# Six small GpSimd loads into a tile without readers, in an attention and GEGLU decode kernel

## The chip, the cores and the metric

The kernel runs on one core of a Trainium2 chip. The metric is device time in microseconds (us). The median of three runs of the kernel before is 188.51 us (188.46 to 188.59). The profile shows one separate execution of the same kernel.

The engines are PE (TensorE, the matrix engine), DVE (VectorE), ACT (ScalarE), POOL (GpSimd) and SP (SyncE). In the profile PEld is PE's weight load, and SPq, POOLq and so on are an engine's sequencer, which waits and issues DMAs. Data moves between the off-chip memory and the on-chip memory (128 partitions) through 16 DMA engines.

## The reference

One decode step of a transformer block for two sequences: a modulation computed from a condition `c`, attention of one query over the last 1024 cached positions with 32 heads of 192, and a gated feed-forward part. Weights, inputs and caches are bf16.

```python
mod = (silu(c) @ w_mod).reshape(2, 6, 1, 640)       # sa, ca, ga, sb, cb, gb
h = layernorm(x) * (1 + ca) + sa
q = (h @ wq).reshape(2, 1, 32, 192).transpose(0, 2, 1, 3)
k, v = k_cache[:, :, -1024:], v_cache[:, :, -1024:]  # each [2, 32, 1024, 192]
p = softmax(einsum('bhqd,bhkd->bhqk', q, k) * 192 ** -0.5)
x = x + ga * (einsum('bhqk,bhkd->bhqd', p, v) reshaped @ wo)
h = layernorm(x) * (1 + cb) + sb
x = x + gb * ((gelu(h @ w_gate) * (h @ w_up)) @ w_down)
```

## The kernel before, in words

The program writes one list of operations for each engine, in the order in which they are declared; a small scheduler (`_Sched`) adds the waits. `S.op` declares a computing operation and `S.dma` a load or a store. Each takes the keys that it reads and writes, and further dependencies in `deps`; from these, `emit` puts semaphore waits (line 93) in front of an instruction. A DMA adds 16 in all to its semaphore when it has landed. All DMAs are declared for SP, and the DMA call itself is the helper `k_dma`, so that all of them carry line 261.

The work goes through these stages:

- The modulation matrix `w_mod` (4800 KB on the page), the small inputs `c` and `x` (eight rows of 320 bytes each, into the tiles `cc` and `xc`), and `wq` in two pieces are loaded. POOL clears some tiles and builds an identity matrix (lines 270 to 281), and after that has no work. The query is computed and broadcast into the tile `qbc`.
- K and V stream through a ring of five slots. A load fills a slot with one tile: 128 partitions of 64 rows of 192, 24,576 bytes in a partition. There are four tiles of K and four of V for each sequence, in the order K of sequence 0; then V of sequence 0 and K of sequence 1 by turns; then V of sequence 1. `declare_ring` declares a load as soon as the slot's previous tile has its last reader, and that reader is what SP waits for.
- A step `(b, t, hf)` handles half a tile of K: DVE multiplies it in place by the query (`d_mul`, line 456), PE sums groups of products with the identity matrix (`p_reduce`, line 467), and DVE adds up the rest (`d_rows`, line 476). PE also runs `filler` products (line 445) whose results nobody reads. After sequence 0's K come its softmax (lines 482 to 499), masks (`d_mask`, line 504) and products with V (`p_pv`, line 516), the latter two in between the steps of sequence 1.
- Then the output projection (`wo`, four loads into the place of `wq`), the second normalisation and the feed-forward part. `w_gate`, `w_up` (two loads) and `w_down` (three loads) go into ring slots, behind the last readers of those.
- The result is stored, and SP's tail waits for the store.

The loop around the change declares the steps; `keep[("red", b, t)]` is the latest `p_reduce` of a tile. The tile `cc` is read once, by the SiLU on ACT (line 351, at 14.5 us in the profile).

Of the kernel before, what the change touches and what calls it, by code (L numbers as in the profile page):

```python
# [103 lines left out]
def bass_adaLN_cond__sliding_block_cached__geglu_ffn__decode_kernel(  # L104
# [15 lines left out]
    P = 128  # L120
# [11 lines left out]
    DN = D // NJ  # L132
# [39 lines left out]
    with es:  # L172
        S = _Sched(nc, es)
# [35 lines left out]
        cc = sb("cc", [P, DN], BF16)  # L209
# [36 lines left out]
        def bank(k):  # L246
            return ("bank", k)
# [8 lines left out]
        sem_wd = [S.sem("d_wd%d" % i) for i in range(len(WD_SPLIT))]  # L256
        sem_ring = [S.sem("d_ring%d" % i) for i in range(NS)]
        sem_out = S.sem("d_out")

        def k_dma(dst, src):  # L260
            return lambda e: e.dma_start(dst, src)  # L261
# [45 lines left out]
        def half_key(slot, hf):  # L307
            return ("ring", slot, hf)
# [4 lines left out]
        keep = {}  # L313
# [16 lines left out]
        def slot_of(*it):  # L330
            return place[it] % NS

        def declare_ring(*consumed, upto=len(items)):
            ring_state["done"].update(place[it] for it in consumed)
            while ring_state["next"] < upto and (ring_state["next"] < NS or (ring_state["next"] - NS) in ring_state["done"]):
                n = ring_state["next"]
                kind, b, t = items[n]
                slot = n % NS
                cache = A_v_cache if kind == "v" else A_k_cache
                S.dma("sp", k_dma(ring[:, slot, :, :].rearrange("p j d -> p (j d)"),  # L340
                                  cache[b, :, K0:Sk, :].rearrange("h (q r) d -> h q r d", q=QP)[:, :, J * t:J * (t + 1), :].rearrange("h q r d -> h q (r d)")),
                      sem_ring[slot], writes=ring_keys(slot), name="ld_%s%d_%d" % (kind, b, t))
                ring_state["next"] += 1
# [107 lines left out]
        def filler(n=1):  # L451
            warm(n * ND, BK_W)

        def d_mul(b, t, hf):
            ks = slot_of("k", b, t)
            S.op("dve", lambda e: e.tensor_tensor(out=ring[:, ks, hf * JH:(hf + 1) * JH, :], in0=ring[:, ks, hf * JH:(hf + 1) * JH, :],  # L456
                                                  in1=qbc[:, b, :].unsqueeze(1).broadcast_to([P, JH, Dh]), op=ALU.mult),
                 reads=["qbc"], writes=[half_key(ks, hf)], name="mul%d_%d_%d" % (b, t, hf))

        def p_reduce(b, t, hf):  # L460
            ks = slot_of("k", b, t)

            def f(e):
                last = None
                o_ap = ps[:, hf, 0:JH * GC].rearrange("p (j c) -> p j c", j=JH)
                for ci in range(NCH):
                    last = e.matmul(o_ap, lhsT=ident_b[:, :], rhs=ring[:, ks, hf * JH:(hf + 1) * JH, ci * GC:(ci + 1) * GC],  # L467
                                    start=(ci == 0), stop=(ci == NCH - 1))
                return last
            keep[("red", b, t)] = S.op("pe", f, reads=[half_key(ks, hf), "ident_b"], writes=[bank(hf)], name="red%d_%d_%d" % (b, t, hf))  # L470
            if hf == 1:
                declare_ring(("k", b, t))

        def d_rows(b, t, hf):
            a = J * t + JH * hf
            S.op("dve", lambda e: e.tensor_reduce(out=S_sb[:, a:a + JH], in_=ps[:, hf, 0:JH * GC].rearrange("p (j c) -> p j c", j=JH),  # L476
                                                  axis=AX.X, op=ALU.add),
                 reads=[bank(hf)], writes=[("S", t, hf)], name="rows%d_%d_%d" % (b, t, hf))
# [24 lines left out]
        def d_mask(b, t):  # L503
            S.op("dve", lambda e: e.tensor_tensor(out=Em[:, t % 2, :, :], in0=E_sb[:, J * t:J * (t + 1)].unsqueeze(2).broadcast_to([P, J, H]),  # L504
                                                  in1=M32b[:, :].unsqueeze(1).broadcast_to([P, J, H]), op=ALU.mult),
                 reads=["E", "M32b"], writes=[("Em", t % 2)], name="mask%d_%d" % (b, t))

        def p_pv(b, t):
            vs = slot_of("v", b, t)
            n = J // 2  # L510

            def f(e):
                last = None
                for jp in range(n):
                    r = 2 * SQ * (jp % 2)
                    last = e.matmul(ps[r:r + 2 * H, BK_O, 0:ON],  # L516
                                    lhsT=Em[:, t % 2, 2 * jp:2 * jp + 2, :].rearrange("p j c -> p (j c)"),
                                    rhs=ring[:, vs, 2 * jp:2 * jp + 2, :],
                                    start=(t == 0 and jp < 2), stop=(t == NTL - 1 and jp >= n - 2), tile_position=(0, r), skip_group_check=True)
                return last  # L520
            keep["pv"] = S.op("pe", f, reads=[("Em", t % 2)] + ring_keys(vs), writes=[bank(BK_O)], name="PV%d_%d" % (b, t))
            declare_ring(("v", b, t))
# [22 lines left out]
            S.op("pe", f, reads=["SEL"] + [("On", b, g) for g in range(NJ)], writes=[bank(BK_H + c) for c in range(NQC)], name="sel%d" % b)  # L545

        steps = [(b, t, hf) for b in range(2) for t in range(NTL) for hf in range(2)]
        for n, (b, t, hf) in enumerate(steps):
            if b == 1 and hf == 0:
                if t == 0:  # L550
                    d_rows(*steps[n - 1])
                    softmax(0)
                d_mask(0, t)
            d_mul(b, t, hf)
            if b == 1 and hf == 0:
                p_pv(0, t)
            filler()
            p_reduce(b, t, hf)
            if n > 0 and not (b == 1 and t == 0 and hf == 0):
                d_rows(*steps[n - 1])  # L560
        normalize(0)
# [24 lines left out]
        for i, (ta, tb) in enumerate(wo_of):  # L586
# [5 lines left out]
              writes=["wg"], deps=r3_dead, name="ld_wg")  # L592
# [72 lines left out]
        with nc.Block() as block:  # L665
            def sp_tail(e):
                e.wait_ge(sem_out, 16)

            @block.sync
            def _(e):  # L670
                S.emit("sp", e, tail=sp_tail)

            @block.gpsimd
            def _(e):
                S.emit("pool", e)

            @block.scalar
            def _(e):
                S.emit("act", e)

            @block.vector
            def _(e):
                S.emit("dve", e)

            @block.tensor
            def _(e):
                S.emit("pe", e)
# [28 lines left out]
```

## Time and profile before

| | |
|---|---|
| median of 3 runs | 188.51 us (188.46 to 188.59) |
| profiled execution, its own time | 188.72 us |
| its span, first to last instruction | 187.0 us |
| instructions in the span | 2330 |
| mean granted clock of PE | 0.896 |
| busy: PE, DVE, ACT, POOL | 126.3, 107.0, 13.9, 4.9 us |
| read from off-chip memory | 76.88 MB, 411 GB/s over the span |
| DMA packets | 4221, of which 500 under 512 bytes |

The profile's page divides the span into 40 equal slices (4.7 us each) and gives the busy share of each engine in tenths, and of the 16 DMA engines together. Its table of queues gives packets, megabytes, and the packets' time as a share of 16 engines' span. The chain of work that ended last is followed back from the last instruction to whatever released each piece. The windows give busy time in chosen stretches, and the timeline single instructions: start in us, length in us, engine, line, operation, output and inputs. Besides these views the trace records every DMA packet (queue, start, length, bytes) and every update of a semaphore by a DMA, so that one load's landing can be seen as up to 16 moments, one for each DMA engine that took part.

### The profile page before, as it was taken

What the parts mean: (1) busy time and instruction counts of PE and PEld (TensorE: products, weight loads), DVE (VectorE), ACT (ScalarE), POOL (GpSimd) and SP (SyncE); (2) the same over time, 40 slices, a digit from 0 to 9 for tenths busy, and PEclk for the clock granted to TensorE, in tenths of its full rate; (3) what the DMA queues carried; (4) which work ended last, traced back from release to release, by engine and by line L of the source; (5) the groups of instructions that cost most, each with busy time, mean ns of one, the idle gap of its engine ahead of it and who ended that gap; (6) DMA issues with size and microseconds to landing.
All of it is one profiled execution on the core that took longest, in us unless ns stands there. A gap on an engine that the chain in (4) does not pass through costs nothing.

```text
span 187.0 us, 2330 instructions
## 1 busy us (share of the span) xinstructions
PE 126.3 (68%) x1039; PEld 62.6 (34%) x1039; DVE 107.0 (57%) x114; ACT 13.9 (7%) x24; POOL 4.9 (3%) x12
## 2 busy tenths in 40 slices
PE   0004542564999899449999829929719999688663
PEld 0001221251443343125454414503315555455321
DVE  6802500029799997399699198296564540744331
ACT  2003300031000000100000000000010001400400
POOL 8100000000000000000000000000000000000000
PEclk9999999558799999957999988975975999999998
DMA  7999899999999999999999999999999999999980
GB/s 263 394 474 426 386 450 424 415 442 457 426 431 417 424 421 426 436 452 431 431 419 421 431 426 421 452 435 431 421 421 431 426 435 429 416 402 437 410 360 27
DMA packets 4221, 77.02 MB, mean 412 GB/s; under 512 B 500, under 2 KB 500, under 8 KB 1140
## 3 DMA queue, kind: packets, MB, share of 16 engines
q1 hardware_dynamic: 4212, 76.88, 96.6%
q8 instruction: 8, 0.13, 0.3%
q14 instruction: 1, 0.01, 0.0%
HBM read 76.88 MB, written 0.00 MB: 411 GB/s over the span
## 4 chain that ended last, share of the span: by engine, by line
DMA 47%; PE 27%; DVE 21%; SPq 2%; issue 1%; ACT 1%; POOL 0%; POOLq 0%; DVEq 0%
DMA ring<-in_A_k_cache_dram 34%; DVE ring L456 14%; DMA ring<-in_B_w_down_dram 13%; PE ps L516 11%; PE ps L467 11%; PE ps L445 3%; DVE Sg L476 3%; DVE Em L504 2%; SPq L261 2%; ACT E_sb L495 1%; DVE M L482 0%; PE ps L497 0%; PE ps L491 0%; DVE gm L486 0%; PE ps L484 0%
## 5 line engine op out<-in xcount | busy, mean ns | idle before, releaser
L456 DVE TENSOR_TENSOR ring<-ring,qbc 128x6144 bf16<-128x6144 bf16 x16 | 53.5, 3351 | 11.6 <-DMA ring<-in_A_k_cache_dram 11.6
L467 PE MATMUL ps<-ring,ident_b 128*128 128x512 bf16 x192 | 49.9, 416 | 12.5 <-DVE ring L456 12.5
L467 PEld LDWEIGHTS ps<-ring,ident_b 128*128 128x128 bf16 x192 | 19.3, 105 | 40.0 <-DVE ring L456 16.3
L516 PE MATMUL ps<-ring,Em 128*64 128x384 bf16 x256 | 26.7, 371 | 4.9 <-DVE Em L504 4.9
L445 PE MATMUL ps<-qbc,ident_b 128*128 128x384 bf16 x145 | 28.8, 331 | 0.7 <-ACT qbc L423 0.7
L504 DVE TENSOR_TENSOR Em<-E_sb,M32b 128x2048 bf16<-128x2048 bf16 x8 | 18.2, 2282 | 4.7 <-PE ps L516 4.7
L516 PEld LDWEIGHTS ps<-ring,Em 128*64 128x64 bf16 x256 | 15.6, 125 | 15.4 <-DVE Em L504 6.4
L445 PEld LDWEIGHTS ps<-qbc,ident_b 128*128 128x128 bf16 x145 | 13.2, 100 | 13.6 <-issue 5.0
L476 DVE TENSOR_REDUCE Sg<-ps 128x32 f32<-128x512 f32 x16 | 11.0, 686 | 9.0 <-PE ps L467 9.0
L392 PE MATMUL ps<-ring,scT 128*32 128x480 bf16 x40 | 4.4, 601 | 15.3 <-DVE scT L349 15.3
L415 PE MATMUL ps<-r,hT 128*32 128x384 bf16 x80 | 6.2, 488 | 9.1 <-DMA r<-in_A_wq_dram 9.1
L425 DVE CAST ring<-ps 128x384 bf16<-128x384 f32 x4 | 2.0, 552 | 15.3 <-PE ps L415 14.4
L415 PEld LDWEIGHTS ps<-r,hT 128*32 128x32 bf16 x80 | 2.9, 135 | 12.5 <-issue 5.8
L530 ACT ACTIVATE On<-ps,rden 32x192 bf16<-32x192 f32 x4 | 1.6, 411 | 73.1 <-PE ps L516 62.3
L392 PEld LDWEIGHTS ps<-ring,scT 128*32 128x32 bf16 x40 | 1.2, 132 | 16.7 <-DVE scT L349 15.3
L611 PE MATMUL ps<-r,ring 128*32 128x160 bf16 x192 | 4.1, 233 | 2.8 <-DVE ring L580 1.1
L534 DVE TENSOR_SCALAR On<-ps,rden 32x192 bf16<-32x192 f32 x4 | 1.7, 417 | 7.4 <-ACT On L530 7.4
L611 PEld LDWEIGHTS ps<-r,ring 128*32 128x32 bf16 x192 | 3.4, 97 | 3.9 <-issue 2.7
L580 DVE STREAM_TRANSPOSE ring<-ring 128x512 bf16<-128x512 bf16 x3 | 4.1, 1424 | 0.1
L495 ACT ACTIVATE E_sb<-Sg,nb 128x256 bf16<-128x256 f32 x2 | 1.0, 508 | 40.2 <-DVE nb L494 40.2
L629 PE MATMUL ps<-ring,hT 128*32 128x384 bf16 x40 | 2.2, 329 | 2.1 <-DMA ring<-in_B_w_up_dram 1.5
L434 PE MATMUL ps<-ring 128*128 128x192 bf16 x16 | 2.7, 361 | 1.2 <-DVE ring L425 1.2
(68 smaller groups left out, 52.4 us busy)
## 6 DMA issues: line engine op xcount, KB each, us to landing
ring<-in_A_k_cache_dram SPq DMA_DIRECT2D x8, 3072.0 KB, 29.9
ring<-in_A_v_cache_dram SPq DMA_DIRECT2D x8, 3072.0 KB, 25.7
r<-in_A_wo_dram SPq DMA_DIRECT2D x2, 2560.0 KB, 37.9
ring<-in_w_mod_dram SPq DMA_DIRECT2D x1, 4800.0 KB, 14.1
r<-in_A_wq_dram SPq DMA_DIRECT2D x1, 4608.0 KB, 23.3
r<-in_A_wq_dram SPq DMA_DIRECT2D x1, 3072.0 KB, 31.3
r<-in_A_wo_dram SPq DMA_DIRECT2D x1, 1920.0 KB, 44.4
ring<-in_B_w_gate_dram SPq DMA_DIRECT2D x1, 1920.0 KB, 16.5
```

The source lines that it names most:

```text
L261: return lambda e: e.dma_start(dst, src)
L392: last = e.matmul(ps[SQ * j:SQ * j + SQ, bk, 0:3 * DN].rearrange("p (i n) -> p i n", i=3), lhsT=scT[:, k, :], rhs=wm_v[:, k, 3 * part * D: ...
L415: last = e.matmul(ps[SQ * j:SQ * j + SQ, BK_H + c, 0:QC], lhsT=hT[:, k, :], rhs=wq_v[:, k, RN * j + QC * c:RN * j + QC * (c + 1)], start=( ...
L445: last = e.matmul(ps[:, bk, 0:2 * Dh], lhsT=ident_b[:, :], rhs=qbc[:, :, :].rearrange("p b d -> p (b d)"), start=True, stop=True)
L456: S.op("dve", lambda e: e.tensor_tensor(out=ring[:, ks, hf * JH:(hf + 1) * JH, :], in0=ring[:, ks, hf * JH:(hf + 1) * JH, :], in1=qbc[:, b ...
L467: last = e.matmul(o_ap, lhsT=ident_b[:, :], rhs=ring[:, ks, hf * JH:(hf + 1) * JH, ci * GC:(ci + 1) * GC], start=(ci == 0), stop=(ci == NC ...
L476: S.op("dve", lambda e: e.tensor_reduce(out=S_sb[:, a:a + JH], in_=ps[:, hf, 0:JH * GC].rearrange("p (j c) -> p j c", j=JH), axis=AX.X, op ...
L495: S.op("act", lambda e: e.activation(out=E_sb[:, :], in_=S_sb, func=ACTF.Exp, scale=SCALE, bias=nb[:, 0:1], accum_out=esum[:, b:b + 1]), r ...
L504: S.op("dve", lambda e: e.tensor_tensor(out=Em[:, t % 2, :, :], in0=E_sb[:, J * t:J * (t + 1)].unsqueeze(2).broadcast_to([P, J, H]), in1=M ...
L516: last = e.matmul(ps[r:r + 2 * H, BK_O, 0:ON], lhsT=Em[:, t % 2, 2 * jp:2 * jp + 2, :].rearrange("p j c -> p (j c)"), rhs=ring[:, vs, 2 * ...
L580: S.op("dve", (lambda t0, nt: lambda e: e.transpose(oT[:, t0:t0 + nt, :], oc.rearrange("p (q k) -> p k q", k=NT)[:, t0:t0 + nt, :]))(t0, n ...
L611: last = e.matmul(ps[SQ * j:SQ * j + SQ, BK_M, 0:DN], lhsT=oT[:, t, :], rhs=wo_v[:, t, DN * j:DN * j + DN], start=(t == 0), stop=(t == NT ...
```

## The change

Behind each of the first six `p_reduce` (sequence 0, tiles 0 to 2, both halves), one small load is declared for POOL. It reads `a` groups of `p` rows from the left 160 columns of `w_down` (a row there is 320 bytes; the groups start 256 rows apart) into the first `a * p` partitions of the tile `cc`, which has no reader any more. The loads have 2, 3, 34, 64, 17 and 1 rows. Each waits for the latest `p_reduce` of its tile, and by the key `pl`, which all six write, for the landing of the small load before it. They share one semaphore, and SP's tail waits for all six.

```diff
+        sem_pl = S.sem("d_pool")
...
+        forms = [(2, 1), (3, 1), (2, 17), (2, 32), (1, 17), (1, 1)]
+
+        def small_load(i, dep):
+            a, p = forms[i]
+            src = B_w_down[0:a * 2 * P, 0:DN].rearrange("(a p) n -> a p n", a=a)[:, 0:p, :]
+            S.dma("pool", k_dma(cc[0:a * p, :], src), sem_pl, writes=["pl"], deps=[dep], name="ld_small%d" % i)
+
         for n, (b, t, hf) in enumerate(steps):
...
             p_reduce(b, t, hf)
+            if n < len(forms):
+                small_load(n, keep[("red", b, t)])
...
             def sp_tail(e):
                 e.wait_ge(sem_out, 16)
+                e.wait_ge(sem_pl, 16 * len(forms))
```

## The prediction

> **What bounds the kernel now.** I read the page first: the forty slices, the queues, the chain.
>
> ```profile
> POOL 8100000000000000000000000000000000000000
> ...
> DMA  7999899999999999999999999999999999999980
> ...
> q1 hardware_dynamic: 4212, 76.88, 96.6%
> q8 instruction: 8, 0.13, 0.3%
> q14 instruction: 1, 0.01, 0.0%
> ...
> DMA 47%; PE 27%; DVE 21%; SPq 2%; issue 1%; ACT 1%; POOL 0%; POOLq 0%; DVEq 0%
> ```
>
> All 16 DMA engines together are busy 96.6% of the span on one queue, and only the first 2 us and the last 3.2 us, after the last load, are empty. GpSimd (POOL) is idle after slice 2. The q8 and q14 rows are instruction fetches, the only other traffic: they matter below, as the one thing this trace shows of a second queue on a busy DMA engine.
>
> Next the windows (columns: length, then busy us of PE, PEld, DVE, ACT, POOL, then granted clock, DMA share, GB/s), for the time in which the small loads will run and for the end:
>
> ```profile
> 50.00:60.00 10.00, 9.39 (x46) 4.16 (x45) 10.00 (x6) 0.00 (x0) 0.00 (x0) 1.00 1.00 428
> 60.00:75.00 15.00, 13.19 (x64) 5.70 (x63) 13.54 (x8) 0.00 (x0) 0.00 (x0) 1.00 1.01 434
> ...
> 175.00:183.50 8.50, 6.01 (x95) 2.60 (x95) 1.41 (x2) 0.49 (x1) 0.00 (x0) 1.00 0.84 345
> ```
>
> From 50 to 75 us the DMA share is 1.00: no hole in which a further transfer could go free. DVE is full there too, but it doesn't set the end, as SyncE's (SP's) timeline and the end of the chain show:
>
> ```profile
> 52.93 0.54 SPq L261 DMA_DIRECT2D ring<-in_A_k_cache_dram  x1
> 60.37 0.54 SPq L261 DMA_DIRECT2D ring<-in_A_v_cache_dram  x1
> 68.11 0.54 SPq L261 DMA_DIRECT2D ring<-in_A_k_cache_dram  x1
> ...
> 157.68 0.33 SPq L261 DMA_DIRECT2D ring<-in_B_w_gate_dram  x1
> ```
> ```profile
> 159.95 23.80 DMA ring<-in_B_w_down_dram
> 183.76 0.04 issue
> 183.80 0.35 PE ps L652 x8
> ```
>
> Each of these loads is issued long before the queue runs dry. By the landing records, the load ahead of the one issued at 52.93 lands at 70.85, the one ahead of 60.37 at 78.16, and the last W_o piece, ahead of 157.68, at 167.7 on its first engine: 18, 18 and 10 us of queued work. So compute may slip by 10 us without a gap, and the end is the last w_down landing (183.76) plus 3.2 us of tail. One ring load takes 7.30 us from landing to landing (39.76, 47.06, 54.36, first engine), which is 8 packets of 914 ns: every DMA engine streams its 8 of the 128 partitions back to back, and time added to one engine stays with it to the end.
>
> The engines aren't level, though. The 16 landings of the last w_down piece are spread over 2.15 us. Behind the latest, the others lie by 0.25, 0.33, 0.34, 0.41, 0.49, 0.61, 1.06, 1.61, and seven by 2.0 or more. A delay counts only by what it exceeds this slack.
>
> **The change, part by part.** Nothing is removed or moved. Added: six POOL DMAs, six POOL waits, and one wait at SP's tail.
>
> *POOL's waits.* Each load waits for a reduction on PE (steps 0 to 5 end near 49.6, 52.9, 56.4, 60.3, 64.2, 68.0) and, through the key "pl", for the landing of the small load before it. Behind these waits stand only the other small loads; no engine reads their tile. Cost 0. SP's tail wait comes after `sem_out`, which lands at 186.59, over 100 us after the sixth load: 0, covered by the whole second half.
>
> *Bytes.* Rows 2, 3, 34, 64, 17, 1: 121 of 320 B, 38,720 B against 76.88 MB. The trace has 24 packets of 320 B (c, x, out) at 19.6 ns. Spread evenly: 121 x 19.6 / 16 = 0.15 us per engine. If a load is split over few engines, as the eight-row loads of c and x are (their semaphores get 5 updates: four engines and one more), 64 rows could be 32 on each of two engines: 32 x 19.6 = 0.63 us there; 17 rows on one: 0.33. Bounds 0.15 and 0.63 for the worst engine. I take the upper, since the c and x rows show a split by four and the source has 2 in its outer dimension.
>
> *Switching queues.* No row shows a small packet of another queue. Lower bound: the semaphore packets of q1 take 9 ns each and the packets beside them keep to 914. Upper bound: the instruction fetches. A 16 KB one at 31.5 us moves one engine's landing from 0.34 to 1.89 us behind the first, 1.55 us; the 8 KB one at 56.8 moves one from 0.15 to 1.10, 0.95 us.
>
> ```profile
> q1 hardware_dynamic: 16, 0.39, 95.5%
> q14 instruction: 1, 0.01, 2.0%
> ```
>
> That is the DMA view for 56.5 to 57.5 us: the fetch itself holds its engine 2.0% of 16 us, 0.33 us, so most of the 0.95 us is not transfer; the q1 packet after it took 1,574 ns for its usual 914. A line through the two fetches gives 0.60 us per 8 KB and 0.35 us at no bytes. So a switch costs between 0.01 and 0.35 us per load and engine. I take 0.35: a fetch on another queue is nearer in kind than a semaphore packet inside the same queue.
>
> Sum for an engine with 32 rows: 0.35 + 0.63 = 0.98 us; with 17 rows 0.68; with a single row 0.37. Eleven engine visits (2 + 3 + 2 + 2 + 1 + 1) fall on sixteen engines. The seven latest have a mean slack of 0.35 us, and at least one of the two 32-row engines is among them with a chance of 1 - (9/16)(8/15) = 0.7. So the end moves by 0.98 - 0.35 = 0.63 us; 0.98 if the very latest is hit, some 0.3 if only a 17-row or single-row engine is late.
>
> How many engines a GpSimd load visits, the trace can't show; its semaphores tell of SP's loads only. [...]
>
> *DVE beside POOL.* Where POOL and DVE worked together in this trace, DVE lost:
>
> ```profile
> 2.03 1.80 POOL L280 MEMSET SEL<- 128x2048 bf16 x1
> ...
> 2.38 3.23 DVE L286 CAST M32b<-M 128x32 bf16<-128x32 f32 x1
> ```
>
> A 128x32 cast took 3.23 us, until POOL's memsets were over (5.57 us). What POOL does for a DMA no row shows; nearest are its instructions, 0.09 to 1.80 us. If each small load held DVE for 1.80 us, the K stage would slip by 10.8 us; the queue's 17 to 18 us there and DVE's own 11.6 us of later waits for K (three waits in the table of waits) cover that. Taken at 0. [...]
>
> Total: 0.63 us. On the profiled execution, 188.72 (span 187.0 and 1.72 around it), that is 189.35; on the median of 188.51, which is 0.21 lower, 189.14; six semaphore packets of 9 ns on an engine make it 189.2.
>
> **The rivals.** *Hidden (not slower).* The switch is free, as between packets of q1, and rows are spread: 0.15 to 0.24 us on the worst engine, partly in its slack. Against it: the fetches; for it: semaphore packets cost 9 ns. 188.5 to 188.8. It decides as long as a load costs a late engine under 0.38 us in all.
>
> *Every engine, six times.* If every load visits all 16 engines at 0.35 us, 6 x 0.36 = 2.15 us go on every engine, slack is no help, and the 32-row engines add 0.63 - 0.35 = 0.28: 188.5 + 2.4 = 190.9. Against it: the four-engine loads of c and x.
>
> *DVE stalled beyond its cover.* If one load holds DVE for a whole multiplication (3.35 us) as well as 1.80, six make 31 us against 17 us of queue; 10 us or more slower. For it stands only the cast row.
>
> *Not what it says.* The loads are chained by landing, and each may land late behind 914 ns packets; then they drift into later tiles. The DMA is as full there, and the price is the same.
>
> **How the numbers follow.** Forecast, few engines and a switch price: 0.42, with 188.9 to 189.6. Hidden: 0.29. Every engine: 0.17, with 190.2 to 191.1 for a switch of 0.25 to 0.37. DVE: 0.03. A gain: 0.09; nothing is taken off any queue, so it could only come from an altered order of fetches on the late engines, where one fetch is worth up to 1.5 us. A measurement of this kernel tells some 0.2% (0.38 us) from no change. Slower: 0.42 + 0.17 + 0.03 = 0.62; same 0.29; faster 0.09. The range, 188.4 to 191.1, leaves out most of the gain and DVE cases and the edges of the others.
>
> **What would show it.** Right: a new queue on the page with some 121 packets of 320 B; POOL instructions at about 50 to 70 us; q1 packets of over 1.2 us beside them; the last w_down landing 0.4 to 1.0 us later; the tail still 3.2 us; multiplications still 3.35 us. Wrong: all 16 landings later by 2 us (every engine visited); the spread of the landings unchanged and the end too (hidden); multiplications over 3.4 us or a DMA share under 0.95 after 75 us (DVE); a changed time outside the span, for which I have no row.

## The result, and the profile after

The change costs 0.7 us: 189.25 us in the median of four runs (188.99 to 189.35) against 188.54 (188.46 to 188.59, four runs) for the kernel before, a ratio of 1.0032 with a 95% interval of 1.0020 to 1.0045. The number was forecast, 189.2. The cause was not: the sum has a price for switching queues that the runs don't show (0.35 us for each load and engine, where `six_2x1` gave 0.02), and lacks a cost that falls on all 16 engines (their last landings moved by 0.49 to 1.15 us).

The page after (span 187.5 us, the execution itself 189.24):

```profile
POOL 8100000000101101011000000000000000000000
...
DMA  7999899999999999999999999999999999999990
...
q1 hardware_dynamic: 4212, 76.88, 96.5%
q8 instruction: 8, 0.13, 0.3%
q0 software_dynamic: 240, 0.04, 0.1%
q14 instruction: 1, 0.01, 0.0%
...
DMA 47%; PE 27%; DVE 21%; SPq 2%; issue 1%; ACT 1%; POOL 1%; DVEq 0%; POOLq 0%
```

The new queue is q0, with 240 packets where 121 rows were to be moved. It holds 0.1% of 16 engines' span by its own account; the end moved by 0.3%.

The windows (same columns as before) and the end of the chain:

```profile
50.00:60.00 10.00, 9.55 (x46) 4.39 (x45) 9.74 (x6) 0.00 (x0) 1.19 (x2) 0.96 1.01 431
60.00:75.00 15.00, 13.19 (x64) 5.74 (x62) 14.15 (x8) 0.00 (x0) 1.34 (x2) 1.00 1.00 421
...
175.00:183.50 8.50, 6.51 (x86) 2.75 (x83) 2.86 (x7) 1.68 (x2) 0.00 (x0) 1.00 0.92 377
```
```profile
158.88 25.40 DMA ring<-in_B_w_down_dram
184.29 0.04 issue
184.33 0.35 PE ps L663 x8
```

In the window from 60 to 75 us the DMA engines are as busy as before (share 1.00, it was 1.01) and move 421 GB/s where it was 434. The last w_down landing goes from 183.76 to 184.29; the tail is still 3.2 us.

GpSimd's own timeline shows the drift that the chain of landings makes:

```profile
50.52 0.68 POOL L262 DMA_DIRECT2D cc<-in_B_w_down_dram  x1 [44.93 <-PE ps L468]
57.68 0.51 POOL L262 DMA_DIRECT2D cc<-in_B_w_down_dram  x1 [6.48 <-PE ps L446]
64.19 0.65 POOL L262 DMA_DIRECT2D cc<-in_B_w_down_dram  x1 [6.00 <-DMA cc<-in_B_w_down_dram]
71.50 0.69 POOL L262 DMA_DIRECT2D cc<-in_B_w_down_dram  x1 [6.66 <-DMA cc<-in_B_w_down_dram]
79.73 0.53 POOL L262 DMA_DIRECT2D cc<-in_B_w_down_dram  x1 [7.54 <-DMA cc<-in_B_w_down_dram]
85.90 0.53 POOL L262 DMA_DIRECT2D cc<-in_B_w_down_dram  x1 [5.63 <-DMA cc<-in_B_w_down_dram]
```

Each small load lands 5.9 to 7.9 us after its issue, so the six spread over 50 to 92 us. Nobody waits for them but the next, and SP's tail long after.

**How the landings moved.** For each big load take the mean of its 16 landings, after less before. It is +0.09 us at the first K load (a later start, before any small load), +0.11 at the load that lands near 62 us, +0.27 near 69, +0.56 near 77, +0.78 near 84, +0.84 near 91, and 0.74 to 0.76 in most of the loads after that (up to 0.87 where an instruction fetch falls between). Net of the start, the six loads cost each DMA engine 0.67 us in the mean. Put in order, the 16 landings of the last load moved by 0.49 to 1.15 us, the earliest by 0.73 and the latest by 0.53: none stayed. That is the prediction's own sign for "every engine visited", at a third of its 2 us. The loads of 2 and 3 rows (50.5 and 57.7) left nothing to see; those of 34 and 64 rows (64.2 and 71.5) did nearly all.

The packet records say what the 240 packets are. The 34 rows come as 2 packets of 13 rows (4,160 bytes) and 2 of 4; the 64 rows as 4 packets of 13 and 2 of 6. So two engines carried 17 and 32 rows each, as predicted. But beside them stand 42 packets of 52 bytes, 14 of 16 and 14 of 24: 13, 4 and 6 times 4 bytes on each of the other 14 engines, the same steps in which the rows come. I call one row, or one piece of 4 bytes, a descriptor. By these lengths, beside the two engines that had 32 rows each, each of the other 14 got 32 descriptors of 4 bytes (packets of 52, 52 and 24 bytes). I call these descriptors filler (they have nothing to do with PE's `filler` products). And 96 of the 4-byte packets are 6 x 16 increments of the semaphore: the landing records have 16 updates for each of the six loads, that of one row too, where SP's loads of c and x have 5.

### The profile page after: what moved, and what is told of

Same layout as the page of the kernel before. It is cut to its first block, busy times and chain, and to the rows that moved or that the text cites. A ratio compares the mean times of both kernels' runs of the same rounds, so it can differ in the third digit from the quotient of the medians.

```text
span 187.5 us, 2342 instructions
## 1 busy us (share of the span) xinstructions
PE 126.7 (68%) x1039; PEld 62.5 (33%) x1039; DVE 107.0 (57%) x114; ACT 13.9 (7%) x24; POOL 8.4 (5%) x18
## 3 DMA queue, kind: packets, MB, share of 16 engines
q1 hardware_dynamic: 4212, 76.88, 96.5%
## 4 chain that ended last, share of the span: by engine, by line
DMA 47%; PE 27%; DVE 21%; SPq 2%; issue 1%; ACT 1%; POOL 1%; DVEq 0%; POOLq 0%
DMA ring<-in_A_k_cache_dram 33%; DVE ring L457 14%; DMA ring<-in_B_w_down_dram 14%; PE ps L517 11%; PE ps L468 11%; PE ps L446 3%; DVE Sg L477 3%; DVE Em L505 2%; SPq L262 2%; ACT E_sb L496 1%; PE ps L498 1%; DVE M L483 0%; PE ps L492 0%; DVE gm L487 0%; PE ps L485 0%
## 5 line engine op out<-in xcount | busy, mean ns | idle before, releaser
L446 PE MATMUL ps<-qbc,ident_b 128*128 128x384 bf16 x145 | 30.1, 343 | 0.7 <-ACT qbc L424 0.7
L446 PEld LDWEIGHTS ps<-qbc,ident_b 128*128 128x128 bf16 x145 | 13.8, 104 | 14.8 <-issue 7.3
L416 PE MATMUL ps<-r,hT 128*32 128x384 bf16 x80 | 6.8, 524 | 8.0 <-DMA r<-in_A_wq_dram 8.0
L262 POOL DMA_DIRECT2D cc<-in_B_w_down_dram x6 | 3.6, 599 | 77.2 <-PE ps L468 44.9
```

Of the source, the lines that this page charges most:

```text
L416: last = e.matmul(ps[SQ * j:SQ * j + SQ, BK_H + c, 0:QC], lhsT=hT[:, k, :], rhs=wq_v[:, k, RN * j + QC * c:RN * j + QC * (c + 1)], start=( ...
L446: last = e.matmul(ps[:, bk, 0:2 * Dh], lhsT=ident_b[:, :], rhs=qbc[:, :, :].rearrange("p b d -> p (b d)"), start=True, stop=True)
```

## The experiments

"Shift" below is the mean landing of the last w_down load, run less before, less the same at the first K load. It comes from one profile each; the ratios are of timed runs, with 95% intervals, against the kernel before on the same chip (188.46, 188.70 or 188.63 us). Every shift lies within the interval of its ratio. Rows and filler descriptors are counted from the packet records.

**1. Which loads.** Two of the six alone, and the other four alone:

```diff
-        forms = [(2, 1), (3, 1), (2, 17), (2, 32), (1, 17), (1, 1)]
+        forms = [None, None, (2, 17), (2, 32)]                        # only_two
+        forms = [(2, 1), (3, 1), None, None, (1, 17), (1, 1)]         # only_four
```

> Only the loads of 34 and 64 rows, at their places. In the changed kernel the mean landing of a load's 16 engines moved by 0.66 us (0.75 after a start that was 0.09 later). Three prices are open. By descriptors (every engine is given as many as the fullest one, 17 and 32 here, about 12 ns each): 49 x 0.012 = 0.60 us, 189.1. By visits (0.11 us for each load on every engine, whatever its size): 0.22 us, 188.75. By bytes (98 of 121 rows): 0.55 us, 189.1.

> Only the loads of 2, 3, 17 and 1 rows. By descriptors (1 + 1 + 2 + 1 on an engine): 0.06 us, 188.6. By visits: 4 x 0.11 = 0.44 us, 189.0. By bytes (23 of 121 rows): 0.13 us, 188.65.

Measured: 189.14 us and a ratio of 1.0036 (1.0023 to 1.0048), shift 0.61, for the two; 188.66 and 1.0011 (1.0002 to 1.0020), shift 0.08, for the four. A price for each load, of any size, is out: four loads cost 0.08 us where it asked 0.44. Descriptors and bytes remain.

**2. Rows or descriptors.** Six equal loads of 64 rows, grouped in two ways:

```diff
+        forms = [(2, 32)] * 6        # six_2x32
+        forms = [(1, 64)] * 6        # six_1x64
```

> Six loads of two groups of 32 rows in the place of the six forms. By descriptors: 6 x 32 x 0.012 = 2.3 us, 190.9. By visits: 0.66 us, 189.2. By bytes (384 rows for 121): 2.1 us, 190.6. By the rows' own packets on two engines for each load, as the prediction had it (32 x 0.02 + 0.35 on two engines, round the 16): about 1 us on each engine at most, 189.5.

> Six loads of one group of 64 rows: rows and bytes as with two groups of 32, but the outer dimension is 64 on both sides, so that 16 engines can have 4 rows each. By descriptors: 6 x 4 x 0.012 = 0.3 us, 188.85. By visits: 0.66 us, 189.2. By bytes: 2.1 us, 190.6.

Measured: 190.96 us, 1.0131 (1.0117 to 1.0145), shift 2.48 for two groups of 32; 189.59, 1.0063 (1.0049 to 1.0077), shift 1.10 for one group of 64. The views of the DMAs from 42 to 100 us, the first of `six_2x32` (335 of its 384 packets, as the sixth load lands later) and the second of `six_1x64` (packets, MB, share; then KB of a load and us to its landing):

```profile
q0 software_dynamic: 335, 0.11, 1.0%
...
cc<-in_B_w_down_dram POOLq DMA_DIRECT2D x6, 20.0 KB, 8.7
```
```profile
q0 software_dynamic: 192, 0.12, 0.7%
...
cc<-in_B_w_down_dram POOLq DMA_DIRECT2D x6, 20.0 KB, 6.4
```

The same 20 KB a load, and more than twice the cost in two groups: bytes alone are out. But one group of 64 costs three times what four descriptors an engine were to cost, so the price by the fullest engine's descriptors falls too. Two prices would fit both, if a row costs the same in either grouping: a row of 320 bytes takes 1.10 x 16 / 384 = 46 ns of engine time, summed over the 16 engines, and filler the rest, (2.48 - 1.10) x 16 / 2688 = 8.2 ns a descriptor.

**3. The two prices apart.** Fewer bytes with the descriptors kept, and fewer filler descriptors with the rows kept:

```diff
-            src = B_w_down[0:a * 2 * P, 0:DN].rearrange(...)
-            S.dma("pool", k_dma(cc[0:a * p, :], src), ...)
+            src = B_w_down[0:a * 2 * P, 0:16].rearrange(...)          # the two narrow kernels, forms as in experiment 2
+            S.dma("pool", k_dma(cc[0:a * p, 0:16], src), ...)
...
+        forms = [(4, 16)] * 6                                         # six_4x16, rows of 320 bytes
```

> Six loads of two groups of 32 rows, with rows of 32 bytes for 320. The runs so far: six loads of this form with 320 bytes moved the mean landing by 2.47 us (0.41 a load), of one group of 64 rows by 1.07 us (0.18 a load). Packets of 4 bytes for each missing row are seen on the 14 engines that have no rows. By descriptors, real or filler, whatever their bytes: 2.3 to 2.5 us again, 190.9. By filler alone (0.41 less the 0.18 of the rows): at least 1.4 us, 189.9 and more, the rest going with the bytes. By bytes alone: 0.25 us, 188.75.

> Six loads of one group of 64 rows with rows of 32 bytes for 320: four descriptors on each of 16 engines and no filler. If the 0.18 us a load there went with the bytes: 0.1 to 0.3 us, 188.7. If with the rows as descriptors, whatever their bytes: 1.07 us, 189.55.

> Six loads of four groups of 16 rows: the same 64 rows of 320 bytes, on four engines with 16 rows each, 16 filler descriptors on each of the other twelve. By the descriptors of the fullest engine (16 for 32): 6 x 0.20 = 1.2 us, 189.7. By rows and filler priced apart (64 rows 0.18 us, 8 ns a filler descriptor on its engine): 6 x (0.18 + 0.10) = 1.7 us, 190.15. By bytes: as with two groups of 32, 190.95.

Measured: 190.63 us, 1.0108 (1.0092 to 1.0123), shift 1.94 for `six_2x32_narrow`; 188.90, 1.0013 (1.0004 to 1.0021), shift 0.30 for `six_1x64_narrow`; 190.18, 1.0080 (1.0066 to 1.0094), shift 1.77 for `six_4x16`. With a tenth of the bytes, the 2 x 32 kernel keeps four fifths of its cost and the 1 x 64 kernel a quarter: filler cost without bytes, and a row's price fell with its bytes (32 bytes: 0.30 x 16 / 384 = 12.5 ns). The third run was forecast at 1.7 us by the two prices; the fullest engine's descriptors gave 1.2 and bytes 2.5.

**4. From which queue.** The six loads of the change, issued by SP between the big loads:

```diff
-            S.dma("pool", k_dma(cc[0:a * p, :], src), sem_pl, writes=["pl"], deps=[dep], ...)
+            o = (0, 2, 5, 39, 103, 120)[i]
+            S.dma("sp", k_dma(cc[o:o + a * p, :], src), sem_pl, writes=[("pl", i)], deps=[dep], ...)
```

> The six loads of the change, issued by SP on the big loads' own queue and without waiting for one another (each into partitions of its own). No filler, if the big queue has none, as with c and x. By the rows' own packets: 121 x 0.02 / 16 = 0.15 us in the mean, up to 1.4 us on one engine (1 + 1 + 17 + 32 + 17 + 1 rows, if the same engine takes the first share each time), so 188.5 to 189.9 by that engine's slack, with most of the other landings where they were. If small rows cost the same from any queue: all 16 landings 0.66 us later, 189.2.

Measured: 188.87 us, 1.0011 (1.0003 to 1.0020), shift 0.33. No queue q0 appears; q1 has 132 packets more than the 4212 of before:

```profile
q1 hardware_dynamic: 4344, 76.92, 96.6%
```

The shift lies between the two forecasts: twice the 0.15 us that the packets' own 20 ns give, half of the change's 0.67. By the row price it is right: 0.33 x 16 / 121 = 44 ns a row on this queue too, summed over the engines. By this sum GpSimd's queue itself added nothing to a row (46 ns in `six_1x64`); its filler did.

The sum isn't what each engine pays. In the records each packet of an engine starts 3 or 4 ns before the one ahead of it ends, so an engine's packets can be followed. In `by_sp` three engines carry 117 of the 121 rows and lose 0.83 to 1.03 us between 46 and 112 us; the eight that carry no row and no instruction fetch lose 0.16 to 0.20 us, in longer packets of the big loads. So, beyond what every engine loses, 17 to 20 ns of a row fall on its own engine, as the first forecast had it; the rest is spread over all 16.

**5. Without the groups, and out of range.** The change with its two large loads as one group each; twice as many rows as in 2 x 32; and six loads of two rows:

```diff
+        forms = [(2, 1), (3, 1), (1, 34), (1, 64), (1, 17), (1, 1)]   # flat
+        forms = [(2, 64)] * 6                                         # six_2x64
+        forms = [(2, 1)] * 6                                          # six_2x1
```

> The change with its two large loads as one group each (34 rows and 64 rows in a row), all six by GpSimd. Prices fitted so far: 45 ns of one engine for a row of 320 bytes, 9 ns for a filler descriptor, nothing for a load as such. By these: 121 rows x 45 / 16 = 0.34 us, and some 30 to 60 filler descriptors, 0.03 us: the mean landing 0.37 us later for the 0.66 of the change, 188.9 to 189.0. If GpSimd's large loads cost by rows alone and the grouping is of no account: 0.66 us again.

> Six loads of two groups of 64 rows: 64 descriptors on every engine, of which 14 engines have filler only. By the fitted prices: 128 x 45 / 16 + 14 x 64 x 9 / 16 = 0.36 + 0.50 = 0.86 us a load, 5.2 us for six, about 193.7. If the filler's price levels off with its number: between 2.5 us (as with 32) and 4, 191.1 to 192.5.

> Six loads of two rows: every load still visits all 16 engines, with one row or one filler descriptor and the semaphore's increment. By the fitted prices: 6 x (2 x 45 + 14 x 9) / 16 = 0.08 us, and 6 x 9 ns of increments, 0.05 us: 0.13 us in all, not to be told from no change in time. By the prediction's price of 0.35 us for each visit to another queue: 2.1 us on every engine, 190.7.

Measured: `flat` 188.90 us, 1.0014 (1.0005 to 1.0023), shift 0.34; `six_2x64` 193.44, 1.0254 (1.0240 to 1.0268), shift 4.72; `six_2x1` 188.71, 1.0005 (0.9995 to 1.0014), shift 0.11. The first halves the cost of the change by its shape alone. The second is 9% under its forecast, and nothing levels off. The third settles the switch: six visits to each of 16 engines cost 0.11 us together, not 2.1.

The shifts beside rows x 44 ns / 16 + filler x 8 ns / 16, with both prices fitted to these runs (us; sums before rounding). The semaphore's increments, some 0.05 us of each engine in every kernel with six GpSimd loads (six packets of 9 ns), have no term of their own:

| kernel | rows | filler | by the two prices | shift measured |
|---|---|---|---|---|
| the change | 121 | 727 | 0.33 + 0.36 = 0.70 | 0.67 |
| only_two | 98 | 686 | 0.27 + 0.34 = 0.61 | 0.61 |
| only_four | 23 | 41 | 0.06 + 0.02 = 0.08 | 0.08 |
| six_1x64 | 384 | 0 | 1.06 | 1.10 |
| six_4x16 | 384 | 1152 | 1.06 + 0.58 = 1.63 | 1.77 |
| six_2x32 | 384 | 2688 | 1.06 + 1.34 = 2.40 | 2.48 |
| six_2x64 | 768 | 5376 | 2.11 + 2.69 = 4.80 | 4.72 |
| by_sp | 121 | 0 | 0.33 | 0.33 |
| flat | 121 | 53 | 0.33 + 0.03 = 0.36 | 0.34 |
| six_2x1 | 12 | 84 | 0.03 + 0.04 = 0.08 | 0.11 |

`six_2x32_narrow` lies outside: 0.30 for its rows and 1.34 for its filler make 1.64, and 1.94 was measured. Its filler came in single packets of 128 bytes, which took 44 ns, where the same 32 descriptors came as 52, 52 and 24 bytes in `six_2x32`. What packet lengths do to the price is not settled.

## Why the prediction was right, and where it was not

*The bound.* Right. The DMA engines have no gap (share 1.01 and 1.00 in the windows from 50 to 75 us), the end is the last w_down landing (184.29), compute has cover (the load ahead of the K load issued at 53.87 us landed at 71.00), and what was added stayed (+0.84 us in the mean landing near 91 us, 0.74 to 0.87 after that).

*Waits, tail, DVE.* Right at zero. The multiplications are the same to a nanosecond, six POOL instructions of 0.5 to 0.7 us beside them (first before, then after):

```profile
L456 DVE TENSOR_TENSOR ring<-ring,qbc 128x6144 bf16<-128x6144 bf16 x16 | 53.5, 3351 | 11.6 <-DMA ring<-in_A_k_cache_dram 11.6
```
```profile
L457 DVE TENSOR_TENSOR ring<-ring,qbc 128x6144 bf16<-128x6144 bf16 x16 | 53.5, 3351 | 10.9 <-DMA ring<-in_A_k_cache_dram 10.9
```

The cast that stood behind the memsets (3.24 us in this profile too) was no guide to a DMA issue.

*Switching queues, 0.35 us a visit.* Wrong: `six_2x1` gives 0.11 us for six loads that each visit all 16 engines, 0.02 us a load, rows included. The line through the 8 KB and 16 KB instruction fetches was read down to no bytes; the 0.35 us that it gives there is not the price of a second queue's visit. The sum's six semaphore packets of 9 ns on an engine had no row of a GpSimd load behind them; the profile after shows them, 16 for each load, at 9 ns.

*Bytes, 19.6 ns a row on the fullest engine.* Near to what a row's own engine pays (17 to 20 ns in `by_sp`), but less than half of what it costs in all, 44 ns a row; the sum had nothing for the other engines. In `six_2x32` the q0 packets lasted 10.7 us summed over the engines, and those of q1's 24,576-byte packets that took over 925 ns ran over their usual 914 by 33.3 us in sum (2.8 before, beside instruction fetches); (10.7 + 30.5) / 16 = 2.6 us, against a shift of 2.48. Three quarters of the price stands in the big queue's packets. For the change itself the same sum is (4.3 + 7.0) / 16 = 0.71 us, against 0.67.

*Which engines.* Wrong where it mattered: the split over two engines was right, but the other 14 got as many descriptors of filler (17 and 32). Followed engine by engine, the nine that had at most six rows and no instruction fetch lost 0.56 to 0.61 us in the change, and the one with 33 rows and no fetch 0.97 us. So most of the cost was level, and the slack of 0.35 us, which the sum subtracted, is no help against that part. The rival "every engine, six times" had the place right, at 0.36 us for each load and engine where 0.67 / 6 = 0.11 was measured, and nearly all of that for two of the six.

So the predicted 0.63 us had a switch price that isn't there and a slack that helps little, and lacked the filler and the half of the row price that falls on the other engines. That it met 0.7 is chance. The signs listed beforehand would have told: all landings moved, and the spread (2.15 us, now 1.94) stayed. Nor did the sign "q1 packets of over 1.2 us beside them" come: of the 24,576-byte packets the longest beside small ones took 1.16 us, and the five over 1.2 us stand beside instruction fetches, as before.

*The drift.* "Not what it says" came true in part, at the price that was named: none.

## What to carry to other kernels

Where the DMA engines are full from end to end (96.6% of the span here), a small load is not free (0.67 us for six loads of 38,720 bytes together), and its shape set its price: count the descriptors of the fullest engine, and for a load from GpSimd charge the other engines as many, at the 8 ns of the fit above. Shape such a load so that its rows spread over more engines (one group of 34 and of 64 rows here, over 12 and 16 engines: 0.34 us for 0.67), or issue it from the big loads' queue. There the few engines with the rows paid most (0.83 to 1.03 us in `by_sp`), and SP's issue of one K load took 5.92 us for 0.54, which the queued work covered here. To find what a DMA cost in such a kernel, compare the landings of all 16 engines load by load, not the packets' own lengths (q0's 4.3 us in sum are 0.27 us an engine) nor one end time (0.53 us later, the mean 0.67).

## What the runs showed of the hardware that was not expected

- A GpSimd load in two groups sent 4-byte descriptors to the engines that had no rows, by the packets' lengths as many as the fullest engine had rows (17 beside the 34 rows, 32 beside the 64). They cost 7.5 to 9.8 ns each, by the shifts of the four kernels with six grouped loads, less their rows.
- A row of 320 bytes cost 44 to 46 ns of engine time, summed over the 16 engines, from either queue, though its packets take 14 to 20 ns a row in the records and the big loads moved 320 bytes in 12 ns (914 ns for 24,576). Why the packets beside it grew is open (33.3 us over their usual 914 ns in `six_2x32`, 2.8 before); it wasn't tried with rows of another pitch, source or target.
- A single row was cut into 16 pieces of 20 bytes, and 17 rows in one group went two by two over nine engines.
- The engines kept their distances: before, the 16 KB instruction fetch at 31.5 us put one engine 1.55 us further behind, and the landings of the K and V loads stayed spread over 1.88 to 1.90 us from 39.76 to 151.20 us.
